# A spectral filter with a gated feed-forward: inputs laid out by partitions, more unread products in the head, maxima through DRAM, and a newly ordered plan

## The chip, the cores and the metric

The kernel runs on one core of one Trainium2 chip. Its engines are TensorE (PE, matrix products, with a weight load PEld that overlaps them), VectorE (DVE), ScalarE (ACT), GpSimd (POOL) and SyncE (SP, which issues DMA transfers). The metric is the device time of one execution in microseconds (us), lower is better.

## The reference

Two branches of one normalised input are multiplied. A is a filter in the frequency domain (a two-dimensional real Fourier transform over 2048 rows and 512 columns, a product with complex weights, the inverse transform). B is a feed-forward part with a rectified gate.

```python
xn = _layernorm(x, axis=-1)                      # x: 1 x 2048 x 512, f32
s  = irfft2(rfft2(xn) * (w_r + 1j * w_i))        # weights 2048 x 257
gate, up = xn @ W_gate, xn @ W_up                # 512 x 1376 each
g  = silu(((gate * (gate > 0)) * up) @ W_down)   # 1376 x 512
out = x + s * g
```

## The kernel before, in words

Every f32 operand of a product is split in two f16 halves, and a product is three passes of f16 (high-high, high-low, low-high; `PASSES`). The scale of each group of weights is a power of two found at run time.

The 2048 rows come as eight chunks of two 128-row tiles (`load_x`, lines 292 to 303). A chunk goes through `stats`, `deviation` and `normalise`. For the first two chunks, x0 and x1, `turn_row` (399) turns each row of tiles on PE by a product with a unit matrix, which is a part of the constants `cS`; ACT copies the high half out and DVE subtracts for the low half. The other chunks are turned by a DMA transpose (`turn`, 372).

The feed-forward part has four blocks c of 512 rows. `product(c, f, i)` (661) is one tile of gate (i = 0) or up (i = 1): feature tile f of eleven, twelve matmuls, into "gu" in PSUM. `rectify` and `hidden` make the f16 halves of the hidden value on ACT and DVE, `down` (720) multiplies by `wds` into "dn", and `gate` is the silu. For block 0 the first three feature tiles are worked in halves: rows of x0 first, rows of x1 later (lines 1033 to 1039). The weights come by seven groups (`load_group`, 480), and each group passes `squares` on ACT, a sum on PE and `group_scale` on DVE, then `group_split`, before a product can use it.

The filter has `first_stage` (455, an s product per chunk, written to DRAM as A_d), eight `fft_chunk`s (767, products y, xx, z, v; written as C_d), and `last_stage` (927, an s product per chunk, then sums on POOL and DVE). `finish` (976) loads the rows of x once more, forms x + s * g, and stores. s, v and y use a part of the PE array; changing between such forms is a cost in the planner (`mode`).

Two maxima over all partitions are needed, one for the down weights (md) and one for the filter (mw). `greatest` (551) takes a column of 128 values, turns it to a row by a product with the unit matrix, reduces it on DVE, and spreads the result to all partitions by a second product.

`keep_busy` (391) puts products on PE at the start whose results nobody reads: 12 steps of three.

The order of the work on each engine is written out by a planner, class `Plan` (71). Each step has an engine, a cost, what it reads and writes, and perhaps a due time, a lead (not earlier than so long before its due time) or a margin. `run` (119) hands due times backwards through the dependencies, then simulates: of the steps that can begin now on an engine it takes the one due first. A step with no due time and no successor has a due time of 1e9 and is taken when nothing else can begin. Buffers are counted by tag (`room`): a step whose buffer isn't free can't begin; "gu", "dn" and "F" have two each in PSUM. The constants at lines 33 to 41 set due times and costs. On the chip each engine works through its list in that order, and semaphores keep the data right. SP's list is the queue of nearly all DMA transfers; a transfer that waits holds those behind it.

```python
T0, DOWN, FIRST, FIRST_STEP, MID, MID_STEP, LAST, LAST_STEP = 10.0, 56.9, 49.0, 16.8, 180.6, 14.5, 265.2, 14.8
```

Of the kernel before, what the change touches and what calls it, by code (L numbers as in the profile page):

```python
# [37 lines left out]
YCOST, VCOST, SCOST, MODE = .63, .59, .6, .095  # L38
BUSY = 12
HURRY, SLOW, SLOW_TO = -1, 1, 20  # L40
# [30 lines left out]
class Plan:  # L71
# [7 lines left out]
    LAG = {"PE": .25, "DVE": .16, "ACT": .18, "POOL": .15, "SP": 2.2}  # L79
# [39 lines left out]
    def run(self):  # L119
# [24 lines left out]
        for _ in steps:  # L144
            best = None
            for e, mine in todo.items():
# [59 lines left out]
def dve(n):  # L206
    return .07 + n / 960
# [23 lines left out]
def kernel(ctx: ExitStack, tc: tile.TileContext, x, wg, wu, wd, wl, ew, sp, c_r, c_d, c_m, c_x, c_s, out):  # L231
    nc = tc.nc
    PS = bass.MemoryType.PSUM
    xr, outr = (t[0].rearrange("(p e n) d -> e p n d", p=N1, n=NE) for t in (x, out))
# [17 lines left out]
    cS = cpool.tile([P, 7 + P], F32, name="cS")  # L252
# [15 lines left out]
    DVE.memset(ones, 1.0)  # L268
    warm = cpool.tile([P, 1], F32, name="warm")
# [21 lines left out]

    def load_x(c):
        tile_of(f"x{c}", "k4", [P, 2, D], F32)
        for e in range(2):
            engine, queue = (("SP", SP), ("ACT", ACT))[c == 0 and e]
            for i in range(2) if c == 0 else [None]:
                rows = slice(2 * c, 2 * c + 2) if i is None else slice(i, i + 1)
                to = slice(0, 2) if i is None else slice(i, i + 1)
                step(engine, .6, lambda e=e, queue=queue, rows=rows, to=to: queue.dma_start(T[f"x{c}"][64 * e:64 * e + 64, to], xr[e, :, rows, :]),
                     writes=[(f"x{c}", e, i)], lead=14 if c else None, kb=256 if i is None else 128, lag=2.2, due=(LOADX[c] + (i or 0) * .01) if c < 2 else None)  # L300

    def x_names(c, i):
        return [(f"x{c}", e, None if c else i) for e in range(2)]
# [68 lines left out]
    def turn(c, lows):  # L372
# [15 lines left out]
        step("SP", 2., run, reads=[(f"x16_{c}", i, h) for i in range(2) for h in range(2)],   # L388
             writes=[(f"xT{c // 2}", j, h) for j in range(2 * (c % 2), 2 * (c % 2) + 2) for h in range(2)], kb=100)
# [90 lines left out]
    def load_group(g):  # L480
        w = sum(fwidth(f) for f in GROUPS[g])
        f0 = GROUPS[g][0] * P
        for i, src in enumerate((wg, wu)):
            tile_of(f"raw{g}_{i}", "k4", [P, 4, 2 * P], F32)
            e, queue = (("SP", SP), ("ACT", ACT))[g == 0 and i]
            step(e, .6, lambda i=i, src=src, queue=queue: queue.dma_start(T[f"raw{g}_{i}"][:, :, :w], src.rearrange("(k p) f -> p k f", p=P)[:, :, f0:f0 + w]),
                 writes=[f"raw{g}_{i}"], lead=12 if g else None, kb=2 * w, lag=2.5, due=LOADS[g])

    def squares(g):
        tile_of(f"m{g}", "m", [P, 4], F32)  # L490
        for j, f in enumerate(GROUPS[g]):
            cols = slice(j * P, j * P + fwidth(f))
            for i in range(2):
# [3 lines left out]
                    reads=[f"raw{g}_{i}"], writes=[("wgu", f, 1, i), (f"m{g}", j, i)])  # L497

    def group_scale(g):
        nf = len(GROUPS[g])  # L500
        tile_of(f"sum{g}", "dn" if g < 2 else "F", [P, 4], F32)
        tile_of(f"p{g}", "p", [P, 2, 4], F32)
        step("PE", .2, lambda: matmul(T[f"sum{g}"][:, :2 * nf], ones, T[f"m{g}"][:, :2 * nf], start=True, stop=True),
             reads=[(f"m{g}", j, i) for j in range(nf) for i in range(2)], writes=[f"sum{g}"])
        step("DVE", .52, lambda: scale_of(T[f"sum{g}"][:, :2 * nf], T[f"p{g}"][:, :, :2 * nf], 9), reads=[f"sum{g}"], writes=[f"p{g}"], port=True)

    def group_split(g):
# [35 lines left out]
        step("DVE", .3, rhos, reads=[f"p{g}"], writes=[("rho", g)])  # L543
# [7 lines left out]
    def greatest(name, col, reads, due):  # L551

        tile_of(f"row_{name}", "F", [P, P], F32)
        tile_of(f"all_{name}", "F", [P, 1], F32)
# [627 lines left out]
```

## Time and profile before

| | |
|---|---|
| median of 3 runs | 417.8 us (417.31 to 418.89) |
| profiled execution | 417.77 us, span 416.0 us |
| instructions in the span | 7674 |
| busy share PE / DVE / ACT / POOL | 97% / 74% / 45% / 11% |
| moved by DMA | 51.72 MB in 41764 packets, of which 16064 under 512 bytes and 24864 under 2 KB |
| mean granted TensorE clock | 0.992 |

The span is the time from the first to the last instruction of the profiled execution. A row in order of time has its start, its length, engine, line, operation, output <- inputs, shape and count; in brackets stands the idle time of the engine before it and what ended that. A chain row has start, length and what. Because the engines' wrappers record every operation, all rows have line 64, and tiles are told apart by their names: gu and dn are products of the feed-forward part, s, y, xx, z, v those of the filter, head the turned rows of x0 and x1, idle the unread products, raw the loaded weights, wgu and wds the split ones. Matmul ends are modelled, and some records can be missing.

### The profile page before, as it was taken

What the parts mean: (1) busy time and instruction counts of PE and PEld (TensorE: products, weight loads), DVE (VectorE), ACT (ScalarE), POOL (GpSimd) and SP (SyncE); (2) the same over time, 40 slices, a digit from 0 to 9 for tenths busy, and PEclk for the clock granted to TensorE, in tenths of its full rate; (3) what the DMA queues carried; (4) which work ended last, traced back from release to release, by engine and by line L of the source; (5) the groups of instructions that cost most, each with busy time, mean ns of one, the idle gap of its engine ahead of it and who ended that gap; (6) DMA issues with size and microseconds to landing.
All of it is one profiled execution on the core that took longest, in us unless ns stands there. A gap on an engine that the chain in (4) does not pass through costs nothing.

```text
span 416.0 us, 7674 instructions
## 1 busy us (share of the span) xinstructions
PE 404.9 (97%) x2997; PEld 214.8 (52%) x2997; DVE 307.2 (74%) x648; ACT 188.4 (45%) x356; POOL 45.7 (11%) x68
## 2 busy tenths in 40 slices
PE   7799999999999999999999999999999999899995
PEld 5686454544444444545555456456455445444554
DVE  3748999999998898335585977897763427899943
ACT  3769863545444259420344335435414336432311
POOL 0000000000000000001130321330330018301300
PEclk9699999999999999999999999999999999999999
DMA  8992211055424787963005145053402189575614
GB/s 204 337 337 60 67 36 50 2 151 55 98 52 100 163 249 221 246 222 116 0 2 166 28 138 165 3 165 84 135 2 52 50 205 212 143 203 137 166 54 101
DMA packets 41764, 51.72 MB, mean 124 GB/s; under 512 B 16064, under 2 KB 24864, under 8 KB 41728
## 3 DMA queue, kind: packets, MB, share of 16 engines
q1 hardware_dynamic: 40880, 50.59, 45.6%
q10 hardware_dynamic: 848, 0.66, 0.6%
q8 instruction: 23, 0.38, 0.4%
q14 instruction: 13, 0.11, 0.1%
HBM read 35.48 MB, written 12.60 MB: 116 GB/s over the span
## 4 chain that ended last, share of the span: by engine, by line
PE 91%; DMA 5%; DVE 1%; ACT 1%; issue 0%; ACTq 0%; SPq 0%; DVEq 0%
PE gu L64 51%; PE dn L64 27%; PE z L64 3%; PE xx L64 3%; PE s L64 2%; DMA xt<-in_x 2%; DMA ct<-C_d 2%; PE y L64 2%; PE v L64 2%; DMA raw<-in_wu 1%; PE head L64 1%; PE dn_3b L64 1%; DVE xT L64 0%; DVE ye L64 0%; ACT xT L64 0%
## 5 line engine op out<-in xcount | busy, mean ns | idle before, releaser
L64 PE MATMUL gu<-xT,wgu 128*128 128x512 f16 (+1 forms) x1032 | 216.0, 367 | 3.4 <-ACT r L64 1.2
L64 PEld LDWEIGHTS <-wgu 128*128 128x128 f16 x1032 | 100.6, 99 | 108.4 <-issue 6.7
L64 PE MATMUL dn<-wds,h 128*128 128x512 f16 (+2 forms) x528 | 115.5, 372 | 0.0
L64 PEld LDWEIGHTS <-h 128*128 128x128 f16 (+1 forms) x561 | 53.7, 98 | 58.3 <-issue 2.5
L64 ACT ACTIVATE h<-h 128x512 f16<-128x512 f32 (+1 forms) x44 | 27.7, 629 | 70.2 <-DVE h L64 70.1
L64 DVE TENSOR_TENSOR h<-gu,r 128x512 f32<-128x512 f32 (+2 forms) x52 | 33.6, 646 | 22.6 <-PE gu L64 21.4
L64 POOL TENSOR_TENSOR po<-tt,tt 128x256 f32<-128x256 f32 x16 | 14.8, 926 | 285.1 <-DVE tt L64 236.8
L64 ACT ACTIVATE r<-gu 128x512 f32<-128x512 f32 (+1 forms) x44 | 26.0, 592 | 20.6 <-PE gu L64 20.3
L64 DVE TENSOR_TENSOR h<-h,h 128x512 f16<-128x512 f32 (+1 forms) x44 | 30.0, 690 | 4.5 <-ACT h L64 4.2
L64 POOL TENSOR_TENSOR ae<-zz 128x128 f32<-128x128 f32 (+1 forms) x32 | 19.3, 636 | 60.9 <-ACT zz L64 47.6
L64 DVE SCALAR_TENSOR_TENSOR tt<-xsp,cw,wt 128x512 f32<-128x512 f32 x32 | 25.2, 849 | 0.0
L64 ACT ACTIVATE g<-dn,cdi 128x512 f32<-128x512 f32 (+1 forms) x16 | 10.6, 673 | 25.1 <-PE dn L64 25.1
L64 DVE TENSOR_TENSOR z<-z,z 128x1024 f16<-128x1024 f32 x8 | 9.8, 1222 | 15.4 <-ACT z L64 15.4
L64 DVE TENSOR_TENSOR sv<-sv,g 128x512 f32<-128x512 f32 (+1 forms) x17 | 10.8, 671 | 9.6 <-ACT g L64 8.9
L64 DVE BATCH_NORM_STATS2 st<-x 128x6 f32<-128x512 f32 x16 | 10.9, 683 | 9.3 <-DMA x<-in_x 9.3
L64 PE MATMUL gu<-xT,wgt 128*64 128x256 f16 (+1 forms) x144 | 17.0, 309 | 0.0
L64 DVE TENSOR_TENSOR a<-y,a 128x1024 f16<-128x1024 f32 x8 | 9.7, 1218 | 8.3 <-ACT a L64 8.3
L64 ACT ACTIVATE wgu<-raw 128x512 f16<-128x512 f32 x20 | 12.4, 622 | 6.5 <-DMA raw<-in_wu 6.4
L64 DVE SCALAR_TENSOR_TENSOR wgu<-raw,p,wgu 128x512 f16<-128x512 f32 x20 | 14.5, 746 | 0.5 <-ACT wgu L64 0.4
L64 DVE TENSOR_TENSOR xt<-xt,sv 128x512 f32<-128x512 f32 (+1 forms) x17 | 11.5, 693 | 4.1 <-DMA xt<-in_x 4.1
L64 ACT ACTIVATE xs<-xs 128x1024 f16<-128x1024 f32 x8 | 8.5, 1058 | 12.6 <-DVE xs L64 12.6
L64 PEld LDWEIGHTS <-wgt 128*64 128x64 f16 (+1 forms) x144 | 9.6, 106 | 7.1 <-issue 1.7
(135 smaller groups left out, 432.5 us busy)
## 6 DMA issues: line engine op xcount, KB each, us to landing
A_d<-t SPq DMA_DIRECT2D x16, 256.0 KB, 3.2
rw<-in_wl SPq DMA_DIRECT2D x8, 512.0 KB, 6.5
wt<-in_wl SPq DMA_DIRECT2D x8, 512.0 KB, 4.7
at<-A_d SPq DMA_DIRECT2D x8, 512.0 KB, 4.6
C_d<-t SPq DMA_DIRECT2D x16, 256.0 KB, 3.3
ct<-C_d SPq DMA_DIRECT2D x16, 256.0 KB, 6.1
xt<-in_x SPq DMA_DIRECT2D x32, 128.0 KB, 3.0
out<-xt SPq DMA_DIRECT2D x30, 128.0 KB, 2.3
```

Source lines behind the costliest of these rows:

```text
L64: return lambda *args, **kw: self.tc.keep_in_program_order(f(*args, **kw))
```

## The change

- Inputs: x, W_gate and W_up are rearranged on the host, so that each partition's part is consecutive in DRAM, and the output is put back in the same way. x rows are loaded with one DMA per chunk (two for x0) in place of two or four, W_gate and W_up with pieces of 2 or 4 KB per partition; a store is one DMA of 128 partitions in place of two of 64. All are issued on SP, none on ACT.
- `after_first`: a POOL copy of one value out of x0 into the next tile; the loads of x1 and of weight groups 1 to 6 wait for it.
- The unit matrix is made on POOL (`affine_select`) instead of loaded, and `turn_row` uses PE transposes.
- `keep_busy`: 79 steps of one product each (was 12 steps of three), with no due time, so that the planner puts them wherever PE would stand. They write to a tile "small" of tag "dn", which also holds the sums of groups 0 and 1.
- `greatest`: the column is written to DRAM, read back as one row spread over all partitions, and reduced on DVE. PE has no part in it.
- The planner: when PE is in a partial-array form, it first takes further such steps that can begin and are due within `JOIN`, the same form first. New constants throughout, a lag of 3.0 for SP, margins (`LATE`) in the last stage, a dearer POOL. Two feature tiles are worked in halves in block 0 instead of three (`HALF`). Folds may begin 67.8 ahead of their due time (was 18.2).

```diff
-T0, DOWN, FIRST, FIRST_STEP, MID, MID_STEP, LAST, LAST_STEP = 10.0, 56.9, 49.0, 16.8, 180.6, 14.5, 265.2, 14.8
-LOADS, LOADX, LOADU = [0.5, 0.7, 3.5, None, None, None, None], [-1.2, 1.0], 4.0
-FOLDS, FOLD_LEAD, MARGIN = ['DVE', 'DVE', 'DVE', 'DVE', 'DVE', 'DVE', 'DVE', 'DVE'], 18.2, 1.83
-HIGH_ACT = {(0, 1), (1, 0), (1, 1), (0, 0)}
-NORM, TURN1 = (('DVE', 'DVE'), ('DVE', 'ACT')), 'PE'
-BUSY = 12
-HURRY, SLOW, SLOW_TO = -1, 1, 20
+T0, DOWN, FIRST, FIRST_STEP, MID, MID_STEP, LAST, LAST_STEP = 1.2, 94.9, 53.3, 17.6, 150.3, 18.1, 292.6, 10.8
+LOADS, LOADX = [4.2, 0, 4.4, None, None, None, None], [-2.7, -0.3]
+FOLDS, FOLD_LEAD, MARGIN = ['DVE', 'DVE', 'DVE', 'DVE', 'DVE', 'DVE', 'DVE', 'DVE'], 67.8, 1.95
+HIGH_ACT = {(0, 1), (2, 1), (0, 0), (3, 1), (2, 0), (3, 0)}
+NORM, TURN1 = (('DVE', 'ACT'), ('DVE', 'ACT')), 'PE'
+BUSY, LATE, PAIR1, PAIR2 = 79, 0.4, 0, 0
+SQUARES, HALF = 32.82, 2
+HURRY, SLOW, SLOW_TO = -2, 1, 20
...
-    LAG = {"PE": .25, "DVE": .16, "ACT": .18, "POOL": .15, "SP": 2.2}
+    LAG = {"PE": .25, "DVE": .16, "ACT": .18, "POOL": .15, "SP": 3.}
...
-                    t, s = min((k for k in at if k[0] <= soon), key=lambda k: (k[1].due, k[1].order))
+                    now = [k for k in at if k[0] <= soon]
+                    if e == "PE" and mode:
+                        now = [k for k in now if 0 < k[1].mode < 3 and k[1].due < k[0] + JOIN] or now
+                    t, s = min(now, key=lambda k: (e == "PE" and k[1].mode != mode if mode else 0, k[1].due, k[1].order))
...
+    POOL.memset(unit, 0.0)
+    POOL.affine_select(out=unit, in_=unit, compare_op=ALU.not_equal, fill=1.0, base=0, pattern=[[-1, P]], channel_multiplier=1)
...
+    def after_first(name, to):
+
+        step("POOL", .3, lambda: POOL.tensor_copy(to(), T["x0"][:, 0, 0:1]), reads=[("x0", 0)], writes=[name, "go"])
+
     def load_x(c):
         tile_of(f"x{c}", "k4", [P, 2, D], F32)
-        for e in range(2):
-            engine, queue = (("SP", SP), ("ACT", ACT))[c == 0 and e]
-            for i in range(2) if c == 0 else [None]:
...
+        if c == 1:
+            after_first(("x1", 0), lambda: T["x1"][:, 0, 0:1])
+        for i in range(1 + (c == 0)):
+            rows = slice(i, i + 1) if c == 0 else slice(0, 2)
+            step("SP", .5, lambda rows=rows: SP.dma_start(T[f"x{c}"][:, rows], x[:, 2 * c + rows.start:2 * c + rows.stop, :]),
+                 writes=[(f"x{c}", i)], lead=14 if c else None, kb=256 * (rows.stop - rows.start), lag=2.2, due=(LOADX[c] + i * .01) if c < 2 else None)
...
-        tile_of("idle", "F", [P, 256], F32)
         w = ones.bitcast(F16)
         for k in range(n):
-            step("PE", .43, lambda: [matmul(T["idle"], w[:, 0:P], w, start=True, stop=True) for _ in range(3)],
-                 writes=["idle"], due=1. + .43 * k, lead=0.)
+            step("PE", .213 if k < 26 else .11, lambda: matmul(T["small"][:, 256:], w[:, 0:P], w, start=True, stop=True), writes=[("small", "idle")])
...
-                matmul(head()[:, cols], T[f"xf{c}"][:, i, cols], cS[:, 7:], start=True, stop=True)
-        step("PE", 1., run, reads=[(f"xf{c}", i), "cS"], writes=[(f"head{c}", i)])
+                PE.transpose(head()[:, cols], T[f"xf{c}"][:, i, cols], unit)
+        step("PE", .45, run, reads=[(f"xf{c}", i)], writes=[(f"head{c}", i)])
...
+            if g == 1 and not i:
+                after_first("raw1_0", lambda: T["raw1_0"][:, 0, 0:1])
+            of = src[:, 4 * P * GROUPS[g][0]:4 * (P * GROUPS[g][0] + w)].rearrange("p (k f) -> p k f", k=4)
+            step("SP", .5, lambda i=i, of=of: SP.dma_start(T[f"raw{g}_{i}"], of),
+                 reads=["go"] if g else [], writes=[f"raw{g}_{i}"], lead=12 if g else None, kb=2 * w, lag=2.5, due=LOADS[g])
...
-        step("PE", .31, lambda: matmul(T[f"row_{name}"][0:1, :], col, cS[:, 7:], start=True, stop=True),
-             reads=["cS", *reads], writes=[f"row_{name}"], due=due, margin=MARGIN)
-        step("DVE", .25, lambda: DVE.tensor_reduce(top[0:1, :], T[f"row_{name}"][0:1, :], axis=AX.X, op=ALU.max),
-             reads=[f"row_{name}"], writes=[f"max_{name}"])
-        step("PE", .31, lambda: matmul(T[f"all_{name}"], ones[0:1, :], top[0:1, :], start=True, stop=True),
-             reads=[f"max_{name}"], writes=[f"all_{name}"], due=due + 2, margin=MARGIN)
+        step("SP", .6, lambda: SP.dma_start(row.rearrange("a p -> p a"), col), reads=reads, writes=[f"row_{name}"], due=due, kb=8, lag=3.)
+        step("SP", .6, lambda: SP.dma_start(rows, row.broadcast_to([P, P])), reads=[f"row_{name}"], writes=[f"rows_{name}"], kb=64, lag=5.2)
+        step("DVE", .22, lambda: DVE.tensor_reduce(top, rows, axis=AX.X, op=ALU.max), reads=[f"rows_{name}"], writes=[f"all_{name}"], due=due + 10)
+        return top
...
-        for e in range(2):
-            step("SP", .6, lambda e=e: SP.dma_start(T[n][64 * e:64 * e + 64], xr[e, :, 2 * c + i, :]), reads=[(sn, 2)], writes=[(n, "x", e)], lead=8, kb=128)
+        step("SP", .5, lambda: SP.dma_start(T[n], x[:, 2 * c + i, :]), reads=[(sn, 2)], writes=[(n, "x")], lead=8, kb=256)
...
-            for e in range(2):
-                engine, queue = (("SP", SP), ("ACT", ACT))[e and c == NCH - 1 and i]
-                step(engine, .6, lambda t=t, cols=cols, e=e, queue=queue: queue.dma_start(outr[e, :, 2 * c + i, cols], t()[64 * e:64 * e + 64]),
-                     reads=[(n, part)], kb=w // 4, due=due, lag=2.2)
+            step("SP", .5, lambda t=t, cols=cols: SP.dma_start(out[:, 2 * c + i, cols], t()), reads=[(n, part)], kb=w // 2, due=due, lag=2.2)
...
-    for h in range(2):
-        for f in range(3):
+        for f in range(HALF):
...
-    for f in range(3, NFT):
+    for f in range(HALF, NFT):
```

More of the change, by code (lines that the diff above doesn't have):

```diff
@@ L251 @@
     cX = cpool.tile([64, 2, 2, 64], F16, name="cX")
-    cS = cpool.tile([P, 7 + P], F32, name="cS")
+    cS = cpool.tile([P, 7], F32, name="cS")
+    unit = cpool.tile([P, P], F32, name="unit")
     sgn = cS[:, 0:1]
@@ L289, in inverse_of @@
         DVE.tensor_scalar(b[:, 1, :], b[:, 0, :], -1.0, float(254 << 23), op0=ALU.mult, op1=ALU.add)
+    def after_first(name, to):
+        step("POOL", .3, lambda: POOL.tensor_copy(to(), T["x0"][:, 0, 0:1]), reads=[("x0", 0)], writes=[name, "go"])
     def load_x(c):
         tile_of(f"x{c}", "k4", [P, 2, D], F32)
-        for e in range(2):
-            engine, queue = (("SP", SP), ("ACT", ACT))[c == 0 and e]
-            for i in range(2) if c == 0 else [None]:
[L297 to L300, printed above, removed]
+        if c == 1:
[4 more added lines that the diff above has]
+                 writes=[(f"x{c}", i)], lead=14 if c else None, kb=256 * (rows.stop - rows.start), lag=2.2, due=(LOADX[c] + i * .01) if c < 2 else None)
     def x_names(c, i):
-        return [(f"x{c}", e, None if c else i) for e in range(2)]
+        return [(f"x{c}", 0 if c else i)]
     def stats(c, q, j):
@@ L481, in load_group @@
         w = sum(fwidth(f) for f in GROUPS[g])
-        f0 = GROUPS[g][0] * P
         for i, src in enumerate((wg, wu)):
[L484 to L487, printed above, removed]
+            tile_of(f"raw{g}_{i}", "k4", [P, 4, w], F32)
+            if g == 1 and not i:
[3 more added lines that the diff above has]
+                 reads=["go"] if g else [], writes=[f"raw{g}_{i}"], lead=12 if g else None, kb=2 * w, lag=2.5, due=LOADS[g])
     def squares(g):
@@ L496, in squares @@
                     junk, T[f"raw{g}_{i}"][:, :, cols], AF.Square, accum_out=T[f"m{g}"][:, 2 * j + i:2 * j + i + 1]),
-                    reads=[f"raw{g}_{i}"], writes=[("wgu", f, 1, i), (f"m{g}", j, i)])
+                    reads=[f"raw{g}_{i}"], writes=[("wgu", f, 1, i), (f"m{g}", j, i)], lead=SQUARES)
     def group_scale(g):
         nf = len(GROUPS[g])
-        tile_of(f"sum{g}", "dn" if g < 2 else "F", [P, 4], F32)
+        if g > 1:
+            tile_of(f"sum{g}", "F", [P, 4], F32)
+        to, name = ((lambda: T[f"sum{g}"]), f"sum{g}") if g > 1 else ((lambda: T["small"][:, 4 * g:4 * g + 4]), ("small", g))
         tile_of(f"p{g}", "p", [P, 2, 4], F32)
-        step("PE", .2, lambda: matmul(T[f"sum{g}"][:, :2 * nf], ones, T[f"m{g}"][:, :2 * nf], start=True, stop=True),
-             reads=[(f"m{g}", j, i) for j in range(nf) for i in range(2)], writes=[f"sum{g}"])
-        step("DVE", .52, lambda: scale_of(T[f"sum{g}"][:, :2 * nf], T[f"p{g}"][:, :, :2 * nf], 9), reads=[f"sum{g}"], writes=[f"p{g}"], port=True)
+        step("PE", .2, lambda: matmul(to()[:, :2 * nf], ones, T[f"m{g}"][:, :2 * nf], start=True, stop=True),
+             reads=[(f"m{g}", j, i) for j in range(nf) for i in range(2)], writes=[name])
+        step("DVE", .52, lambda: scale_of(to()[:, :2 * nf], T[f"p{g}"][:, :, :2 * nf], 9), reads=[name], writes=[f"p{g}"], port=True)
     def group_split(g):
@@ L542, in rhos @@
                                      T[f"p{g}"][:, 1, 1:2 * nf:2], op0=ALU.mult, op1=ALU.mult)
-        step("DVE", .3, rhos, reads=[f"p{g}"], writes=[("rho", g)])
+        step("DVE", .3, rhos, reads=[f"p{g}"], writes=[("rho", g)], lead=25)
     def weights(f, i):
@@ L620, in filter_scale @@
              reads=[("mw", q) for q in range(NCH + 2)], writes=["mwt"])
-        greatest("mw", mw[:, NCH + 2:NCH + 3], ["mwt"], due)
+        all_mw = greatest("mw", mw[:, NCH + 2:NCH + 3], ["mwt"], due)
         p = cpool.tile([P, 2, 1], F32, name="pw")
@@ L626, in run @@
         def run():
-            scale_of(T["all_mw"], p, 0)
+            scale_of(all_mw, p, 0)
             inverse_of(p)
@@ L952, in put @@
         def put(e, op, to, a, b, n, reads, write, port=True):
-            eng, cost = ((DVE, dve(n)), (POOL, pool(n)))[e == "POOL"]
-            step(e, cost, lambda: getattr(eng, op)(to(), a(), b()), reads=reads, writes=[write], port=port)
+            eng, cost = ((DVE, dve(n)), (POOL, pool(n) + .2))[e == "POOL"]
+            step(e, cost, lambda: getattr(eng, op)(to(), a(), b()), reads=reads, writes=[write], port=port, margin=LATE)
         def copy(to, of, reads, write):
-            step("ACT", .11, lambda: ACT.activation(to(), of(), AF.Copy), reads=reads, writes=[write])
+            step("ACT", .11, lambda: ACT.activation(to(), of(), AF.Copy), reads=reads, writes=[write], margin=LATE)
         copy(lambda: ac()[:, :, 64:65], lambda: a0()[:, :, 64:65], [zn], (aen, 4))
```

34 lines of the change are left out of this document (18 added, 16 removed).

## The prediction

> **What bounds the kernel now.** I read the shares of busy time first, then the chain of work that ended last, then the instructions of the head in order of time, then windows by stage. The first row is the page's busy time of each engine; the second fence is the chain (start, us, what).
>
> ```profile
> PE 404.9 (97%) x2997; PEld 214.8 (52%) x2997; DVE 307.2 (74%) x648; ACT 188.4 (45%) x356; POOL 45.7 (11%) x68
> ```
>
> ```profile
> 10.25 3.67 PE head L64 x16
> ...
> 16.40 5.65 PE gu L64 x35
> 22.05 0.12 PE sum L64 x2
> 22.17 1.33 PE gu L64 x12
> 23.50 1.79 PE head L64 x16
> 25.29 2.73 PE gu L64 x25
> 28.05 5.29 PE gu L64 x47
> ...
> 65.88 0.31 PE row_md L64 x2
> ...
> 68.88 0.31 PE all_md L64 x2
> ...
> 172.80 0.31 PE row_mw L64 x2
> ...
> 175.94 0.31 PE all_mw L64 x2
> ...
> 359.10 0.78 PE s L64 x24
> ...
> 411.25 0.48 ACT g L64
> ```
>
> PE is the bound: from 16.40 to the last product at 411.23 (just ahead of ACT g) PE works with one gap. So the time has three parts: a head of 16.4 us, a PE stream, and a tail of 416.0 - 411.2 = 4.8 us. Anything off PE counts only if it makes PE wait. The profiled execution took 417.77 us, a span of 416.0 and 1.77 around it; the median of the runs is 417.8, so a sum made against the one needs no shift for the other. I count a difference of 0.5%, 2.1 us, as the least that a measurement of this kernel can tell.
>
> The head has its own reasons. These rows are from the instructions in order of time, the answer on the tile idle, and one-microsecond windows (length, then busy us of PE, its weight loads, DVE, ACT, POOL; granted clock; DMA share; GB/s):
>
> ```profile
> 1.05 6.90 PE L64 MATMUL idle<-ones 128*128 128x256 f16 x36 [1.05 <-DVE md L64]
> L64 PE MATMUL idle<-ones x36: 272/421/421, 1.1 to 7.7; 128*128 128x256 f16 x36
> 6.78 0.69 DVE L64 BATCH_NORM_STATS2 st<-x 128x6 f32<-128x512 f32 x1 [1.28 <-DMA x<-in_x]
> 8.02 0.63 ACT L64 ACTIVATE wgu<-raw 128x512 f16<-128x512 f32 x1 [5.79 <-DMA raw<-in_wu]
> 13.12 0.69 DVE L64 BATCH_NORM_STATS2 st<-x 128x6 f32<-128x512 f32 x1 [1.86 <-DMA x<-in_x]
> 11.00:12.00 1.00, 1.00 (x7) 1.00 (x6) 0.22 (x2) 1.00 (x3) 0.00 (x0) 0.50 1.16 214
> 18.00:19.00 1.00, 1.00 (x7) 0.69 (x6) 0.97 (x5) 0.81 (x3) 0.00 (x0) 0.50 1.04 385
> ```
>
> Row 1 of x0 is there at 6.78, the first weights at 8.02. ACT, which works in order, stands 5.79 us before those weights, and the square root of x0 is queued behind them. After the unread products stop at about 7.9, PE falls to half speed around 11 and, after the next gap, around 18. That is why the first 35 real products take 5.65 us where at full clock 12 take 1.33 (0.111 each, so 3.9).
>
> **The change part by part.** *Head, the main term.* The loads become 2 KB or more of consecutive bytes per partition, only x0 and the first weights are loaded until x0's first row has landed, f32 products with a unit matrix become transposes, and 79 single unread products replace 36. These 79 are real PE time, so they set a floor. They and the first two scale sums share a "dn" buffer of which there are two; product (0, f=1, i=1) needs the second buffer beside (0, f=1, i=0), so in any order that the planner can write, all 79 stand ahead of the fourth half product. Their cost: the 36 began over 1.1 to 7.7, thus 6.6 us from first to last, most at half speed; 43 more at the full-clock 0.111 make 4.8, together 11.4. The floor for reaching the state that before has at 25.29 (four half products, x1 turned) is then 1.05 + 11.4 + transposes of x0 + two sums of 0.12 + 4 x 1.33 + transposes of x1. No row shows an f32 transpose. Upper bound: the eight f32 products that it replaces, 1.79 at full clock. Lower bound: eight f16 128x128 products by the z row below, 1.34 / 24 = 0.056 each, 0.45. I take the middle, 0.9, since neither row is nearer. Floor: 1.05 + 11.4 + 0.9 + 0.24 + 5.32 + 0.9 = 19.8.
>
> TensorE: Matmul & The Clock Gate, section Terms, of the Trainium skill says that trn2's transpose mode is four times faster for FP32; by that page the pair would cost 0.9 instead of 1.8 and an estimated floor would be 18.9. No run here shows it yet.
>
> Can the inputs keep up with the floor? A window from x0's first row to the end of x1's turn, three rows in order of time or of the chain, and two of the DMA issues (KB each, us to landing):
>
> ```profile
> 4.58:28.00 23.42, 19.40 (x132) 16.27 (x131) 15.84 (x48) 13.71 (x36) 0.00 (x0) 0.85 1.08 318
> 23.14 0.88 DVE L64 TENSOR_SCALAR wgu<-raw,p 128x512 f16<-128x512 f32 x2
> 23.93 1.41 DVE L64 SCALAR_TENSOR_TENSOR wgu<-raw,p,wgu 128x512 f16<-128x512 f32 x2
> 207.33 1.34 PE z L64 x24
> raw<-in_wg SPq DMA_DIRECT2D x3, 256.0 KB, 7.2
> x<-in_x SPq DMA_DIRECT2D x14, 256.0 KB, 4.5
> ```
>
> DVE (third pair of columns) worked 15.84 us between the first row of x and the end of x1's turn at 28.0. At least 0.88 + 1.41 = 2.3 of that is for the third weights, which are not yet needed. From 4.6 on, without a wait, that is 4.6 + 13.5 = 18.1, 1.7 short of the floor. The loads that now wait for x0 (a POOL copy releases them; behind it on SP stand x1, the second and third weights and all later loads) are issued from about 4.6 in place of 2.6; with 7.2 us to landing, the slowest of the two rows, they land at 12, ahead of the old 13.12. So the floor is nearest; I add 0.8 for the turn of x1, a chain PE, ACT, DVE that DVE cannot run without gaps, and take 20.6: a gain of 25.3 - 20.6 = **4.7**. Ends: 5.5 (the floor) and 0 (everything as late as before); a loss would need inputs later than now, which fewer and longer pieces exclude.
>
> The clock row first: half speed around 11 and 18, each time some 3 us after PE had gone idle. The same page of the Trainium skill, section Part 1, has a free-running window of about 3.4 us after which an idle PE is halved and a busy one released; the trace agrees (11 and 18 are two such windows apart). By that rule the cold part of the unread products may last one window more or less in another execution, an estimate of 1.7 us either way, which no run here shows.
>
> *Maxima through DRAM.* Four PE pieces of 0.31 go: **1.24**. In their place a column goes to DRAM and a row comes back to all partitions, and DVE reduces it. Rows of the DMA issues, of SP's waits (us in total, times, longest), of the order of time and of the chain:
>
> ```profile
> E_d<-edge SPq DMA_DIRECT2D x2, 8.0 KB, 2.6
> SPq L64 <- DVE t L64: 148.1, 13, 24.2
> 61.69 0.17 DVE L64 TENSOR_REDUCE md<-md 128x1 f32<-128x11 f32 x1
> 70.16 0.23 DVE L64 TENSOR_SCALAR scd<-rho,pd 128x11 f32<-128x11 f32 x1
> 79.28 20.83 PE dn L64 x96
> 193.75 3.20 DVE L64 SCALAR_TENSOR_TENSOR tt<-xsp,cw,wt 128x512 f32<-128x512 f32 x4
> ```
>
> Two small transfers by the nearest row are 2 x 2.6 plus two issues of 0.6, some 6.4 us; now the way from the maximum to the scales takes 70.2 - 61.7 = 8.5. The waiting DMA holds SP, and behind it loads of x and stores of A_d; SP does stand up to 24.2 us for one tile. The cover: the first down product is at 79.28, nine us after the scales, part of which the casts of the weights need, and the filter's scale is first used at 193.75, 18 us after all_mw. I count 0; with the cover gone it costs what SP is late, and that would be the first "dn" of PE standing.
>
> *The one gap of PE in the stream.* The chain's row of the late xt, then PE in order of time:
>
> ```profile
> 344.36 7.82 DMA xt<-in_x
> 355.06 2.75 PE L64 MATMUL gu<-xT,wgu 128*128 128x512 f16 x12 [1.24 <-ACT r L64]
> 342.88 1.51 PE L64 MATMUL s<-ct,cR 64*64 64x257 f16 x48
> 344.33 2.76 PE L64 MATMUL gu<-xT,wgu 128*128 128x512 f16 x12
> ```
>
> DVE waits for a late xt, ACT behind DVE, PE behind ACT for 1.24. One DMA per row instead of two, a margin in the planner's costs and a longer lag for SP speak for its going; a newly written order can bring a like wait elsewhere. Ends 1.24 and -1.24; I take half the gain, **0.6**.
>
> *Joined small products.* Two s groups together take 344.33 - 342.88 = 1.45, against 2 x 0.78: 0.11 per join. With pairs of s alone, six more joins are to be had, with y and v pairs perhaps eight more. Ends 0 and 1.5; **0.5**, about five joins.
>
> *Nothing for:* the unit matrix made on POOL (idle in the head, needed only at x0's transposes), the earlier folds (they fill DVE's waits), the longer due times, and the last store: one DMA on SP instead of two on two queues, the same chain ACT, DVE, DMA; bounds +-0.5.
>
> Sum: 4.7 + 1.24 + 0.6 + 0.5 = 7.0, and 417.77 - 7.0 = **410.7 us**. Ends of the terms together: 417.77 - (5.5 + 1.24 + 1.24 + 1.5 + 0.5) = 407.8 and 417.77 - 1.24 + 1.24 + 0.5 = 418.3.
>
> **The rivals.**
>
> *The clock falls again.* If the first weights come later than the plan has them, PE stands behind 79 spent products and drops to half speed. One stretch of 3.4 us costs 1.7, the wait ahead of it at least as much: 3.3 less, **414.0**. For it: two such stretches now. Against it: the products are spread over all waits.
>
> *DVE becomes the bound.* Windows again, DVE the third busy column:
>
> ```profile
> 28.00:60.00 32.00, 31.96 (x200) 18.54 (x202) 27.23 (x69) 26.56 (x65) 0.00 (x0) 1.00 0.31 87
> 60.00:160.00 100.00, 100.00 (x622) 46.50 (x611) 93.77 (x238) 48.96 (x82) 0.00 (x0) 1.00 0.43 100
> 342.46:412.64 70.18, 67.52 (x504) 35.28 (x501) 55.65 (x99) 24.02 (x63) 18.42 (x30) 1.00 0.60 149
> ```
>
> Between 28 and 160 DVE is busy 121.0 of 132 us. A PE that comes 4.7 earlier leaves 127.3, 95% busy; if it can't be packed closer than now, the head's gain and the 0.6 are given back: 417.77 - 1.24 - 0.5 = **416.0**. Against it: PE never waits there now.
>
> *Slower: the spectral chain ends the kernel.* The last first stage is due at 53.3 + 7 x 17.6 = 176.5 in place of 49 + 7 x 16.8 = 166.6, and eight chunks and the last stages hang on it. If the last stages begin 9.9 later, DVE has its 55.65 us from 342.46 on still to do, from 352.4 to 408.0 without a gap; with half of the present gaps, (70.18 - 55.65) / 2 = 7.3, to 415.3, and with the 3.4 behind it in the span and 1.77 around it **420.5**. It decides once the first last stage is later than about 349. Against it: a due time only ranks steps, and joining takes small stages early.
>
> *All terms at their good end:* about **408**.
>
> **How the numbers follow.** Forecast 0.55, all good 0.12, clock 0.13, DVE 0.12, spectral chain 0.08. The time is the forecast's, 410.7. The range runs from 406.5 (1.3 below the good end, for the unpriced transposes and a shorter cold start) to 416.0, which leaves out the slower case and a little more. Faster by over 0.5% are the forecast, the good end and the clock case: 0.80; DVE's case is within 0.5%: 0.12; slower 0.08.
>
> **What would show it.** Right: half products of rows 2 and 3 from about 20.6, granted clock full from about 8 on, no row_ or all_ on PE, longer s groups, the gap at 355 gone. Wrong: PE idle between the last unread product and the first gu, half clock beyond 8, PE waiting on DVE between 30 and 160, or DVE busy after PE's last product by more than now.

## The result, and the profile after

The changed kernel takes 408.75 us (median; 408.16 to 408.9 over four runs) against 417.74 (417.31 to 418.89) for the kernel before in the same set of runs: a ratio of 0.978, with a 95% interval of 0.9756 to 0.980. The profiled execution took 408.87 us, its span 407.1. The forecast was 410.7; the gain is 9.0 us where 7.0 was summed.

The page's busy shares, and the chain of work that ended last (start, us, what):

```profile
PE 401.4 (99%) x2992; PEld 211.5 (52%) x2992; DVE 304.0 (75%) x647; ACT 188.0 (46%) x358; POOL 46.7 (11%) x72
```

```profile
1.05 7.58 PE small L65 x47
8.66 0.17 DVE p L65
...
10.96 1.23 ACT wgu L65 x4
...
12.85 2.62 PE gu L65 x24
...
17.46 0.89 PE head L65 x8
...
18.37 1.09 ACT xT L65 x2
...
20.83 18.24 PE gu L65 x107
...
68.06 1.44 PE s L65 x48
...
180.84 1.99 PE y L65 x105
...
333.02 1.44 PE s L65 x48
...
356.84 1.44 PE s L65 x48
...
403.06 0.48 ACT g L65
```

From 20.83 to 403.03 the chain is PE alone. In the head it is PE too, but for two stretches, 8.66 to 12.18 and 18.37 to 20.79, where it runs through DVE and ACT, which prepare the weights and the turned rows. So DVE and ACT hold nearly six us of the head's path. row_md, all_md, row_mw and all_mw are no longer on it. The rows at 68 and later show s groups of 48 where before had 24. At 355, where PE stood for 1.24, there is nothing: in the instructions of PE in order of time, only one wait is left after the first matmul of rows 2 and 3.

```profile
1.05 6.42 PE L65 MATMUL small<-ones 128*128 128x256 f16 x38 [1.05 <-DVE md L65]
7.46 0.38 PE L65 MATMUL small<-m,ones 128*128 128x2 f32 x2
...
8.46 1.04 PE L65 MATMUL head<-unit,xf 128*128 128x128 f32 x8
...
12.69 2.78 PE L65 MATMUL gu<-xT,wgu 128*128 128x256 f16 x24
...
18.86 1.58 PE L65 MATMUL gu<-xT,wgu 128*128 128x256 f16 x13
20.83 8.53 PE L65 MATMUL gu<-xT,wgu 128*128 128x256 f16 x62 [0.39 <-DVE xT L65]
```

The first 24 half products take 2.78 us, the full pace of 0.111 each; before, 35 took 5.65. The windows (length, then busy us and count of PE, its weight loads, DVE, ACT, POOL; granted clock; DMA share; GB/s) show when the clock came: 18 matmuls in the 3.3 us up to 5.3, 31 in the 3.4 us behind it. At 18, where the granted clock was 0.50 before, it is 1.00; DVE (third pair) works 86.47 of the 100 us from 60 to 160.

```profile
2.00:5.30 3.30, 3.30 (x18) 2.32 (x17) 1.71 (x5) 0.22 (x2) 0.30 (x2) 1.00 0.97 319
5.30:8.70 3.40, 3.40 (x31) 2.88 (x30) 1.43 (x8) 2.24 (x6) 0.00 (x0) 1.00 0.90 287
18.00:19.00 1.00, 0.94 (x11) 0.73 (x9) 0.61 (x5) 0.63 (x2) 0.00 (x0) 1.00 1.03 385
60.00:160.00 100.00, 100.00 (x637) 47.02 (x638) 86.47 (x221) 52.75 (x89) 0.00 (x0) 1.00 0.49 142
```

The span splits in three. *Head*, up to four half products done and x1 turned: 20.72 in place of 25.29, 4.57 gained. In the changed kernel rows 2 and 3 begin there (20.83, less one of their matmuls that ran ahead of the wait); before, with three feature tiles in halves, two more half products of x0's rows came first, so that its rows 2 and 3 began only near 28. *PE's stream*: from there to the last product 382.31 (to 403.03) in place of 385.94 (25.29 to 411.23), 3.63 gained. *Tail*: 407.1 - 403.03 = 4.07 in place of 4.77, 0.70 gained. Together 8.9, the difference of the spans.

The maxima through DRAM were hidden, but by less than was thought. Two rows of the DMA issues (KB each, us to landing), one of SP's waits (us in total, times, longest), and two of DVE in order of time:

```profile
rows_mw<-row_mw SPq DMA_DIRECT2D x1, 64.0 KB, 4.6
...
row_mw<-mw SPq DMA_DIRECT2D x1, 0.5 KB, 7.3
```

```profile
SPq L65 <- DMA row_md<-md: 8.9, 1, 8.9
```

```profile
143.77 0.75 DVE L65 TENSOR_TENSOR xs<-eo 128x256 f32<-128x256 f32 x2
...
148.19 0.24 DVE L65 COPY wt<-spw 128x4 f32<-128x4 f32 x2 [2.25 <-DMA wt<-E_d]
```

A column of 512 bytes takes 7.3 us to land, and for the first maximum SP stands 8.9 us. It is not the sending that is long, nor other traffic: the trace has the packets of the first column between 51.04 and 51.24, its sixteen completions between 55.6 and 59.4, and the DMA engines 2% busy from 50.3 to 59.4. A 2 KB read issued just behind the second column (wt from E_d) makes DVE wait 2.25.

### The profile page after: what moved, and what is told of

Same layout as the page of the kernel before. It is cut to its first block, busy times and chain, and to the rows that moved or that the text cites. A ratio compares the mean times of both kernels' runs of the same rounds, so it can differ in the third digit from the quotient of the medians.

```text
span 407.1 us, 7606 instructions
## 1 busy us (share of the span) xinstructions
PE 401.4 (99%) x2992; PEld 211.5 (52%) x2992; DVE 304.0 (75%) x647; ACT 188.0 (46%) x358; POOL 46.7 (11%) x72
## 4 chain that ended last, share of the span: by engine, by line
PE 97%; ACT 1%; DVE 1%; issue 0%
PE gu L65 55%; PE dn L65 27%; PE s L65 3%; PE z L65 3%; PE xx L65 3%; PE small L65 2%; PE y L65 2%; PE v L65 2%; PE dn_3b L65 1%; ACT xT L65 1%; ACT wgu L65 0%; PE head L65 0%; DVE xT L65 0%; PE sum L65 0%; DVE p L65 0%
## 5 line engine op out<-in xcount | busy, mean ns | idle before, releaser
L65 PE MATMUL gu<-xT,wgu 128*128 128x512 f16 (+1 forms) x1008 | 213.3, 369 | 0.4 <-DVE xT L65 0.4
L65 PEld LDWEIGHTS <-wgu 128*128 128x128 f16 x1008 | 97.5, 98 | 107.5 <-issue 3.5
L65 POOL TENSOR_TENSOR ae<-zz 128x128 f32<-128x128 f32 (+1 forms) x32 | 17.8, 593 | 62.8 <-ACT zz L65 47.9
L65 DVE TENSOR_TENSOR t<-v,t 128x1024 f16<-128x1024 f32 x8 | 9.8, 1219 | 7.9 <-ACT t L65 7.9
L65 ACT ACTIVATE z<-z 128x1024 f16<-128x1024 f32 x8 | 8.2, 1024 | 15.2 <-PE z L65 15.2
L65 POOL TENSOR_TENSOR pf<-tt,tt 128x256 f32<-128x256 f32 x16 | 14.0, 888 | 7.7 <-PE gu L65 7.7
L65 ACT ACTIVATE p<-pf 128x1024 f16<-128x1024 f32 x8 | 8.4, 1056 | 13.0 <-DVE pf L65 13.0
```

The costliest lines, as they stand in the source:

```text
L65: return lambda *args, **kw: self.tc.keep_in_program_order(f(*args, **kw))
```

## The experiments

Each edit is made to the changed kernel, and the time beside it is the changed kernel's 408.75. The three sets of runs had medians of before between 417.35 and 418.14, so differences of well under a microsecond are read from positions in the traces, not from medians; e5 to e8 ran on another chip than the rest. Positions scatter too. In the changed kernel, e7, e8, e10 and e11, whose heads are worked the same way, the first 38 unread products take 5.96 to 6.79 us, part of them at half pace, and the first sum behind them (the row at 7.46 above) begins at 7.23 to 7.67, held by those products or by the first weights. Rows 2 and 3 follow 13.3 to 13.4 us behind that sum in each, at 20.61 to 20.97. A difference of 0.3 us in that start therefore shows nothing by itself.

**e1: no unread products.**

```diff
-BUSY, LATE, PAIR1, PAIR2 = 79, 0.4, 0, 0
+BUSY, LATE, PAIR1, PAIR2 = 0, 0.4, 0, 0
```

> The changed kernel without any of the 79 unread products (they are no part of the result); the planner writes nearly the same order otherwise. Theory A (they keep the clock): the granted clock falls to 0.5 for one or two stretches of 3.4 us while the turned rows and the first half products run, as it did in the kernel before, so 1.7 to 3.4 us more than 408.75: 410.4 to 412.2. Theory B (they are only PE time and set the start): the first half products begin earlier than 12.85 and the time is 408.0 or less. Theory C (inputs alone set the start): 408.7, the same.

Measured: 414.91 us (413.27 to 418.4), 6.2 more. PE in order of time:

```profile
12.46 0.59 PE L65 MATMUL small<-m,ones 128*128 128x2 f32 x2 [2.39 <-ACT wgu L65]
12.91 5.28 PE L65 MATMUL gu<-xT,wgu 128*128 128x256 f16 x24
...
23.19 1.03 PE L65 MATMUL gu<-xT,wgu 128*128 128x256 f16 x8 [0.94 <-DVE xT L65]
```

The same 24 half products take 5.28 us, half pace throughout, as were the eight turns before them (1.94), and rows 2 and 3 begin 2.4 us later. So the theory on the clock has its direction, and its size in the head, but not in the whole time (410.4 to 412.2). The other 3.8 us come later: the plan, made anew, has the first maximum's column go out at 57.8 (50.2 in the changed kernel), its 8.95 us to landing and the loads of x behind it are on the chain, and PE waits 1.3 for wds and 0.7 for an s; the rest was not parted. Half pace from 12.9 to about 18, some 5.1 us, lies between one and two of the windows of 3.4 us that the Trainium skill gives (TensorE: Matmul & The Clock Gate, Part 1).

**e2: the unread products in a buffer of their own**, of the same tag; the order of all engines unchanged.

```diff
+    tile_of("idle", "dn", [P, 256], F32)
-... matmul(T["small"][:, 256:], w[:, 0:P], w, start=True, stop=True), writes=[("small", "idle")])
+... matmul(T["idle"], w[:, 0:P], w, start=True, stop=True), writes=["idle"])
```

> The changed kernel with the unread products written to a buffer of their own, no longer to the one that holds the sums of weight groups 0 and 1; every engine's order is the same. Theory A: DVE read the first sum only at 8.66, though it was written at 7.84, because it waited for seven unread products that went into the same buffer; DVE was free from 8.22, so the head gets 0.4 us shorter, 408.3. Theory B: DVE was late for another reason, and its read stays at 8.66: 408.75.

Measured: 408.39 us (408.12 to 408.77), span 406.7. DVE's first scale in the changed kernel, and then in e2:

```profile
8.66 0.16 DVE L65 TENSOR_SCALAR p<-small 128x2 f32<-128x2 f32 x1 [0.44 <-PE small L65]
```

```profile
7.88 0.16 DVE L65 TENSOR_SCALAR p<-small 128x2 f32<-128x2 f32 x1
```

In the changed kernel DVE, which reads the sum, waits 0.44 us for unread products written to the same tile behind that sum. With an own buffer it doesn't wait: that part of theory A is shown. Rows 2 and 3 begin at 20.51 and the span is 0.4 shorter, but this is not shown to come from the buffer. The 38 unread products took 5.94 us here in place of 6.42, so the first sum begins at 7.08 in place of 7.46, and rows 2 and 3 follow 13.4 us behind it as before; PE has a wait for DVE there that the changed kernel doesn't have (0.23 us at 12.48). By medians alone the two kernels can't be told apart.

**e3: the POOL copies don't hold the loads back** (they write to a spare tile instead of the next one).

```diff
...
-        step("POOL", .3, lambda: POOL.tensor_copy(to(), T["x0"][:, 0, 0:1]), ...
+        step("POOL", .3, lambda: POOL.tensor_copy(junk1, T["x0"][:, 0, 0:1]), ...
```

> The changed kernel with the POOL copies written elsewhere, so that x1 and the later weights no longer wait for x0; the order on PE, DVE, ACT and SP is the same. Theory A (holding back helps): x0 and the first weights share the DMA engines with x1, land 0.5 to 1 us later (the first square after 6.5 in place of 5.97) and the time is 409.2 to 409.8. Theory B (the larger pieces alone did it): the first square stays within 0.2 of 5.97 and the time within 0.3 of 408.75.

Measured: 409.08 us (408.78 to 409.28). The first weights' square begins at 6.05 (5.97 in the changed kernel), as in theory B, and rows 2 and 3 at 21.12, 0.29 later. But the 38 unread products took 6.96 us here, and the first sum stands behind them at 7.85; from there to rows 2 and 3 it is 13.3 us as in the changed kernel. So no effect of holding the loads back is shown.

**e4: W_gate and W_up in their old layout in DRAM.**

```diff
-            of = src[:, 4 * P * GROUPS[g][0]:4 * (P * GROUPS[g][0] + w)].rearrange("p (k f) -> p k f", k=4)
+            of = src.rearrange("(k p) f -> p k f", p=P)[:, :, P * GROUPS[g][0]:P * GROUPS[g][0] + w]
...
```

> The changed kernel with W_gate and W_up in their old layout in DRAM (512 or 1024 bytes in a row), loads in the same order. Theory A (the layout brought the early start): the first weights land some 2 us later, as in the kernel before (first square about 8.0 in place of 5.97), ACT keeps the square root behind it, and the time is 1.5 to 2.5 longer: 410.3 to 411.3. Theory B (holding back and order did it): within 0.5 of 408.75.

Measured: 411.85 us (411.41 to 412.03), 3.1 more (2.5 in the profiled execution), but hardly in the head: the first weights' square begins at 6.12 (5.97 in the changed kernel), rows 2 and 3 at 21.07. DVE and PE in order of time:

```profile
148.66 0.76 DVE L65 TENSOR_TENSOR xs<-eo 128x256 f32<-128x256 f32 x2 [4.57 <-DMA A_d<-t]
...
150.61 2.75 PE L65 MATMUL gu<-xT,wgu 128*128 128x512 f16 x12 [1.45 <-ACT r L65]
...
162.11 0.85 PE L65 MATMUL s<-xs,cR 64*64 64x257 f16 x24 [0.44 <-DVE t L65]
```

The xs that ran at 143.77 without a wait now waits 4.57 us for a store of A_d, which went out just ahead of the second maximum's column, and PE stands behind it twice. The store was issued at 139.26 and took 9.31 us. Of its sixteen completions eleven are there by 142.91, the others trail to 148.56 among those of the column. So both theories on the head fall, and e6 and e12 ask on.

**e5: the turns of x0 and x1 as f32 products with the unit matrix again**, same order.

```diff
-                PE.transpose(head()[:, cols], T[f"xf{c}"][:, i, cols], unit)
+                matmul(head()[:, cols], T[f"xf{c}"][:, i, cols], unit, start=True, stop=True)
```

> The sixteen turns of x0 and x1 (four for each of four rows) are f32 products with the unit matrix again, in the same order; nothing else differs. Theory A (the turns stand on the path of the head, as the prediction had it: twice four of them for each of two chunks ahead of the first products of rows 2 and 3): eight take 1.79 in place of the 0.89 of the changed kernel, so rows 2 and 3 begin 1.3 to 1.8 us later than 20.8, and the kernel takes 410.0 to 410.6 us. Theory B (DVE sets the head, the turns are hidden under its work): rows 2 and 3 begin within 0.4 of 20.8 and the kernel takes 408.6 to 409.3 us.

Measured: 410.18 us (409.48 to 410.82), 1.4 more. PE in order of time:

```profile
8.39 1.95 PE L65 MATMUL head<-unit,xf 128*128 128x128 f32 x16
...
17.81 1.95 PE L65 MATMUL head<-unit,xf 128*128 128x128 f32 x16
...
22.25 7.02 PE L65 MATMUL gu<-xT,wgu 128*128 128x256 f16 x55 [0.39 <-DVE xT L65]
```

Each chunk's turn takes 0.91 longer, and rows 2 and 3 begin 1.42 later. The turns stand on the path of the head: theory A.

**e6: e3 and e4 together.**

```diff
...
-        step("POOL", .3, lambda: POOL.tensor_copy(to(), T["x0"][:, 0, 0:1]), ...
+        step("POOL", .3, lambda: POOL.tensor_copy(junk1, T["x0"][:, 0, 0:1]), ...
-            of = src[:, 4 * P * GROUPS[g][0]:4 * (P * GROUPS[g][0] + w)].rearrange("p (k f) -> p k f", k=4)
+            of = src.rearrange("(k p) f -> p k f", p=P)[:, :, P * GROUPS[g][0]:P * GROUPS[g][0] + w]
...
```

> The old layout of W_gate and W_up in DRAM, and the two POOL copies no longer hold the loads of x1 and of the later weights back, both together. Each alone moved the first weights' square by 0.15 us or less. Theory A (either of the two is enough to let the first weights through early; with both undone they queue behind the rest as before): first square near 8.0 us in place of 6.0, rows 2 and 3 at 22 to 24 us, kernel 412.5 to 416 us. Theory B (the early first weights are due to something else, such as fewer DMA issues ahead of them or the order of the queue): first square before 6.5 us and a time within 1 us of the 411.9 of the old layout alone.

Measured: 411.31 us (410.6 to 411.86). ACT and PE in order of time:

```profile
5.69 0.63 ACT L65 ACTIVATE wgu<-raw 128x512 f16<-128x512 f32 x1 [3.46 <-DMA raw<-in_wg]
...
21.04 8.31 PE L65 MATMUL gu<-xT,wgu 128*128 128x256 f16 x61 [0.39 <-DVE xT L65]
```

Theory B. DVE waits for A_d as in e4 (4.12). The first weights are early without the new layout of the weights and without the hold: 5.69 against 8.02 before. What all these kernels keep is x by partitions with two transfers for x0 in place of four, no load of the unit matrix, and the first weights on SP, issued at 1.64 and 2.11 (2.57 and, on ACT, 2.28 before). Which of these does it wasn't tried apart.

**e7: loads of xt and stores of the output as two transfers each**, all on SP, same order.

```diff
-... SP.dma_start(T[n], x[:, 2 * c + i, :]) ...
+... [SP.dma_start(T[n][64 * e:64 * e + 64], x[64 * e:64 * e + 64, 2 * c + i, :]) for e in range(2)] ...
-... SP.dma_start(out[:, 2 * c + i, cols], t()) ...
+... [SP.dma_start(out[64 * e:64 * e + 64, 2 * c + i, cols], t()[64 * e:64 * e + 64]) for e in range(2)] ...
```

> Each row of xt is again loaded by two transfers of 64 partitions, and each store of the output is two transfers, all on SP in the same order; the layout is the new one. Theory A (it was the single transfer per row that ended the gap of PE at 355, and SP's queue is near its limit in the last part): DVE waits for xt again, PE stands 0.5 to 1.5 us in all after 330, and the kernel takes 409.3 to 410.5 us. Theory B (the planner's margin and order ended it): PE stands nowhere after 330, and the kernel takes 408.5 to 409.3 us.

Measured: 409.59 us (408.67 to 409.69), 0.8 more. The end of the chain and the span:

```profile
403.09 0.48 ACT g L65
...
404.06 0.42 DVE xt L65
```

```profile
core 0: 407.9 us, clock 0.997
```

PE waits nowhere after 20.95, and its last product ends as in the changed kernel; the 0.8 us lie wholly behind it: 407.9 - 403.07 = 4.83, the tail of before. So the gap at 355 did not go because of the single transfers (theory B on that), but the shorter tail did come from them, which neither theory had counted. The 0.76 is clear of the scatter: the other eleven edited kernels, which all store with one transfer, have tails of 3.99 to 4.42 us.

**e8: the maxima through PE again** (the old `greatest`), planned anew.

```diff
+        step("PE", .31, lambda: matmul(T[f"row_{name}"][0:1, :], col, unit, start=True, stop=True), ...
+        step("DVE", .25, lambda: DVE.tensor_reduce(top[0:1, :], T[f"row_{name}"][0:1, :], axis=AX.X, op=ALU.max), ...
+        step("PE", .31, lambda: matmul(T[f"all_{name}"], ones[0:1, :], top[0:1, :], start=True, stop=True), ...
...
```

> The two maxima go through PE again (a product with the unit matrix, a reduction, a product with ones), as before the change; the planner orders the rest anew. Theory A (the four pieces of 0.31 are real time of PE and nothing else was gained or lost): 1.24 us more, 409.6 to 410.4 us. Theory B (the small transfers hold SP and cost something that PE's way does not): the kernel takes 408.9 us or less.

Measured: 410.95 us (410.57 to 411.37), 2.2 more, above theory A's 409.6 to 410.4. Two rows of the chain of the changed kernel, and the same work in e8 around the second maximum:

```profile
146.34 5.18 PE gu L65 x24
151.52 1.29 PE dn L65 x6
```

```profile
147.20 0.31 PE row_mw L65 x2
147.51 5.29 PE gu L65 x24
152.79 0.31 PE all_mw L65 x2
153.10 1.40 PE dn L65 x6
```

Each piece of 0.31 also makes the work behind it 0.11 longer (24 gu take 5.29 for 5.18, 6 dn 1.40 for 1.29). PE waits nowhere after 20.97, and its last product ends at 404.85, so the stream from there is 1.67 us longer, four times 0.42. Of the other 0.4 of the span 0.14 lies in the head and 0.28 in the tail.

**e9: 60 unread products, in the buffer of their own** (on top of e2, same order; the last 19 emit nothing).

```diff
+... matmul(T["idle"], w[:, 0:P], w, start=True, stop=True) if k < 60 else None, writes=["idle"])
```

> As the run with the unread products in a buffer of their own, in the same order on every engine, but the last 19 of the 79 unread products are left out (9 of the 24 behind the turn of x0, and the 10 behind them); they write nothing that is read. Theory A (as the prediction had it: the 79 are time of PE that sets a floor for the head): rows 2 and 3 begin 1 to 2.1 us (19 x 0.111) earlier than the 20.5 of that run, and the kernel takes 406.3 to 407.5 us. Theory B (the floor and the work of DVE and ACT on the inputs end at the same time): PE waits in their place, rows 2 and 3 begin between 20.0 and 20.7, and the kernel takes 408.0 to 408.8 us; with the clock falling behind the wait it would be 1 to 3 us more.

Measured: 408.24 us (408.0 to 408.48), span 406.2. PE in order of time:

```profile
11.81 0.38 PE L65 MATMUL small<-m,ones 128*128 128x2 f32 x2 [0.75 <-ACT wgu L65]
12.06 2.89 PE L65 MATMUL gu<-xT,wgu 128*128 128x256 f16 x24
...
20.07 3.11 PE L65 MATMUL gu<-xT,wgu 128*128 128x256 f16 x27 [0.94 <-DVE xT L65]
```

Of 2.1 us of products taken away 0.44 comes out in the start of rows 2 and 3 against e2, or 0.74 when both are counted from the first sum (7.38 here, 7.08 in e2). For the rest PE waits: 0.60 for ACT ahead of that sum, then 0.75 for ACT and 0.94 for DVE, where e2 has 0.23 and 0.39 for DVE. Theory B: PE's floor and the work on the inputs end within a microsecond of each other. The clock stays full behind the short waits. By the runs neither e9 nor e2, the two lowest times, can be told from the changed kernel.

**e10: the planner's old choice of the next step.**

```diff
-                    now = [k for k in at if k[0] <= soon]
-                    if e == "PE" and mode:
-                        now = [k for k in now if 0 < k[1].mode < 3 and k[1].due < k[0] + JOIN] or now
-                    t, s = min(now, key=lambda k: (e == "PE" and k[1].mode != mode if mode else 0, k[1].due, k[1].order))
+                    t, s = min((k for k in at if k[0] <= soon), key=lambda k: (k[1].due, k[1].order))
```

> The planner chooses the next step of PE by due time alone, as before the change, so that s products come in 14 groups in place of 10 and y in 8 in place of 7; all else as in the changed kernel, planned anew. Theory A (a join is worth 0.11 us and no more): five joins lost, 0.5 to 0.6 us, the kernel takes 409.0 to 409.7 us. Theory B (the choice also moves steps so that waits come or go): PE waits after 30 us show in the trace, and the kernel takes 410.5 us or more.

Measured: 412.16 us (412.05 to 412.74), 3.4 more. PE's waits after the head:

```profile
83.88 2.81 PE L65 MATMUL dn<-wds,h 128*128 128x512 f16 x11 [0.45 <-DVE wds L65]
...
162.80 0.85 PE L65 MATMUL s<-xs,cR 64*64 64x257 f16 x24 [1.06 <-DVE t L65]
```

Theory B: 1.5 of the 3.1 us by which PE's stream is longer are two waits that came with the new order. The chain runs through the column of the first maximum (9.37), its row (4.34) and a transposing transfer (6.49). The five joins lie in the other 1.6, which the trace doesn't part further.

**e11: SP's lag, the margin and POOL's cost in the last stages as before**, planned anew.

```diff
-    LAG = {..., "SP": 3.}
+    LAG = {..., "SP": 2.2}
-BUSY, LATE, PAIR1, PAIR2 = 79, 0.4, 0, 0
+BUSY, LATE, PAIR1, PAIR2 = 79, 0., 0, 0
-            eng, cost = ((DVE, dve(n)), (POOL, pool(n) + .2))[e == "POOL"]
+            eng, cost = ((DVE, dve(n)), (POOL, pool(n)))[e == "POOL"]
```

> The planner's lag for SP is 2.2 again (3.0 in the changed kernel), its margin in the last stages 0 (0.4), and POOL's sums there cost 0.2 less, all as before the change; planned anew. Theory A (these margins ended the wait of PE at 355 us): PE waits 0.5 to 1.5 us on DVE or ACT after 330 us, the kernel takes 409.3 to 410.5 us. Theory B (another order or other due times ended it): no wait of PE after 330, the kernel takes 408.4 to 409.2 us.

Measured: 411.14 us (410.19 to 411.53), 2.4 more. PE's waits after the head:

```profile
162.00 0.85 PE L65 MATMUL s<-xs,cR 64*64 64x257 f16 x24 [1.35 <-DVE t L65]
...
181.57 0.87 PE L65 MATMUL y<-cm,at 64*128 64x64 f16 x48 [0.89 <-DMA at<-A_d]
```

Neither theory. No wait comes back after 330, so these constants alone did not end the gap at 355; but two waits of 2.24 us in all come at 162 and 182, where SP's transfers are late.

**e12: the old layout of the weights with the maxima on PE** (e4 and e8), in the order of e8.

```diff
-            of = src[:, 4 * P * GROUPS[g][0]:4 * (P * GROUPS[g][0] + w)].rearrange("p (k f) -> p k f", k=4)
+            of = src.rearrange("(k p) f -> p k f", p=P)[:, :, P * GROUPS[g][0]:P * GROUPS[g][0] + w]
+        step("PE", .31, lambda: matmul(T[f"row_{name}"][0:1, :], col, unit, start=True, stop=True), ...
...
```

> The old layout of W_gate and W_up, as in the run of it alone, and the maxima through PE as in the run of that alone, in the order of the latter. The old layout alone cost 3.1 us, all of it at 143 to 162 us, where DVE waited 4.6 us for a store of A_d that had gone out just ahead of the column of the second maximum. Theory A (the column's store, 128 pieces of 4 bytes, holds up what goes out beside it, and the layout only moved the times): without it no wait of DVE on A_d of over 1 us near 145, and the kernel takes 410.5 to 411.6 us, within 0.7 of the maxima on PE alone. Theory B (the layout itself slows transfers there): the wait and the 3 us stay, the kernel takes 413 to 415 us.

Measured: 411.14 us (411.06 to 411.25), 0.2 above e8. DVE in order of time:

```profile
144.86 0.75 DVE L65 TENSOR_TENSOR xs<-eo 128x256 f32<-128x256 f32 x2
...
149.50 0.22 DVE L65 COPY wt<-spw 128x4 f32<-128x4 f32 x2
```

No wait on A_d, nor on wt. PE's stream is as long as in e8 (383.87 and 383.88). Rows 2 and 3 begin 0.24 later, but the 38 unread products took 7.05 us here in place of 6.13, so that this is not shown to come from the layout. Where no column of single values goes out, the old layout costs nothing that these runs can tell; where it does, 3.1. So the layout of the weights is nearly nothing by itself, and e4's loss belongs to the column's store together with it: theory A. What is shown is the pairing; as the order here is that of e8 and not of e4, and as the trace doesn't show why the old layout brought the A_d store to land behind the column's, that part stays open.

## Why the prediction was right, and where it was not

*PE bounds, and the parts are head, stream and tail: right.* 4.57 + 3.63 + 0.70 = 8.9, against 4.7 + 2.34 + 0. In the head, though, the bound is not PE alone.

*Head, 4.7: measured 4.57.* All 79 products stand ahead of the fourth half product, as argued (38 + 7 + 24 + 2 + 5 + 2 + 1). The turn of eight was put at 0.9; the chain has 0.89. The Trainium skill's factor of four for f32 transposes (TensorE: Matmul & The Clock Gate, section Terms), by which it would have been 0.45, is not what was seen: 0.89 against the 1.79 of the products is a factor of two. e1 shows that the clock was the danger and that the products remove it.

But "they set a floor" was only half the cause. By the floor, 19 products less had to give 2.1 us, and e9 gave 0.44 (0.74 from the first sum); the inputs' chain ends nearly with the floor, not 1.7 ahead of it as the window of DVE's work had it. The step that failed is to count DVE's busy time as if it could run without waits for ACT and PE; the chain goes through ACT and DVE in turn. So the near hit of 4.7 is in part luck. With 19 products fewer, rows 2 and 3 still wait until 20.07. So the 0.8 that was added for the turn of x1 stood for something real, but it belongs to the inputs' own end and not on top of the floor. e5 fits with that, as the turns lie on both paths. The reason given for early inputs, fewer and longer pieces of the weights and held-back loads, is not borne out: undoing the one (e4, e12), the other (e3) or both (e6) moves the head by no more than its scatter. The first weights do come two us earlier, and what brings them stays open among the parts that were not undone. The cold part of the unread products does vary, as the prediction allowed for: the same 38 products take 5.72 to 7.05 us over all kernels that have them.

*Maxima, 1.24: the mechanism was right, the term undersized.* e8 puts the stream at 1.67. The missing 0.43 is what the pieces cost the work behind them, 0.11 each. The price of the new way was wrong by far: 2.6 us for a small transfer, taken from an 8 KB store, where the column took 7.3 and 8.9 until SP went on. The cover held in the changed kernel. But "I count 0" is true only of this order: in e1 and e10 the first column is on the chain and PE waits for wds, and the stretch behind the second maximum is where e4, e6, e10 and e11 have most of their waits.

*The gap, 0.6: measured 1.24.* It is gone whole; half was taken out of caution. Of its reasons, the single transfers (e7) and the margin and lag (e11) are each refuted as the cause by itself, as undoing either brings no wait back after 330; the two were not undone together. The new due times and their order and the layout of x remain, and were not taken apart, so the cause stays open.

*Joins, 0.5: about 0.7.* The instructions count s in 10 groups for 14 and y in 7 for 8, five joins as forecast, and 3.63 - 1.24 - 1.67 leaves 0.72. As a remainder over all else that the new order does, that is an estimate. By the rows, a join of two s groups saves 2 x 0.78 - 1.44 = 0.12, so five of them some 0.6.

*The last store, "nothing", bounds 0.5: wrong.* It is worth 0.70, outside its own bounds, and e7 gives it back. One transfer of 128 partitions is not "the same chain": with two, the tail is 4.83 us.

*The rivals.* The clock fell again only when the products were taken away: 414.9, with 414.0 forecast for it, though 3.8 of the 6.2 us had another cause; that the two numbers lie so near is chance. DVE did not become the bound: its busy time from 60 to 160 fell to 86.47, and PE waits for it once, in the head. The spectral chain was not late: the first last stage stands at 333.02, well ahead of 349. The good end, 408, came nearest; the terms that lifted the time from 410.7 towards it are the gap (0.64), the tail (0.70), the neighbours of the maxima (0.43) and the joins (0.2).

## What to carry to other kernels

Count a short piece on a saturated engine with what its interruption costs the work behind it, and price a store by a row of its own kind: 128 values of four bytes took 6.4 us and more here, 8 KB in pieces of 64 bytes 2.0 to 4.7 over all runs. That the small pieces are the reason is likely but was not tried apart. Where two floors end together, taking time from one of them buys little (e9), while taking it from what both share buys most of it (e5: 1.42 of 1.82). Compare a small shift first with the same position in kernels that leave that part alone. A layout or a margin that was put in for one place may earn its keep in another: undo it alone and look where the time is lost, then undo it together with the suspect.

## What was not expected of the hardware

- A store of 512 bytes as 128 pieces of four held the transfers beside it: 7.3 us to landing, a 2 KB read behind it landed only 6.6 us after its issue at 141.53, and in e4 a store of A_d ahead of it took 9.31 us. Without the column the same read landed 2.7 us after its issue in e8 and 2.4 in e12, by the completions in their traces, and the A_d stores there 3.0 to 3.7.
- The granted clock in the profile can miss a slow stretch. In e1 the window of the 24 half products at half pace reads 1.00; the spacing of the matmuls shows it. The trace's record of the clock begins only at 18.45 us there, with full speed:

```profile
13.00:18.00 5.00, 5.00 (x26) 3.57 (x25) 4.58 (x14) 4.68 (x15) 0.00 (x0) 1.00 1.03 408
```

- DVE, reading a sum, waited for later writes by PE to other columns of the same tile (0.44 us in the changed kernel, gone in e2). Whether the chip or the semaphores that the program sets make it wait, no run here shows.
